# Weights loaded in double pieces, last stores moved behind a branch, and small start-up work moved between engines, in an RWKV-5 plus tanh-shrink kernel

## The chip, the cores and the metric

The program runs on one core of a Trainium2 chip. The core has five engines with queues of their own: TensorE (PE; its weight loads are shown as PEld), VectorE (DVE), ScalarE (ACT), GpSimd (POOL) and SyncE (SP). Loads and stores (DMAs) are issued from the queues of SP, ACT and POOL, and carried out by sixteen DMA engines that the queues share. The metric is the device time of one execution in microseconds (us), lower is better. A profile is of one execution, and its span is a little shorter than the execution's time.

## The reference

Two blocks follow each other. The first is a recurrence over 768 time steps for 4 batches and 8 heads of 48 columns; the second takes its output as 3072 tokens of 384 columns, multiplies by `w_in`, applies `h - tanh(h)`, and multiplies by `w_out`.

```python
state = np.zeros((B, H, D, D), dtype=np.float32)
for t in range(S):
    kt, vt, rt = (k[:, :, t], v[:, :, t], r[:, :, t])
    cur = np.einsum('bhd,bhe->bhde', u[None] * kt, vt)
    y[:, :, t] = np.einsum('bhd,bhde->bhe', rt, state + cur)
    state = w[None, :, :, None] * state + np.einsum('bhd,bhe->bhde', kt, vt)
x = np.ascontiguousarray(y.transpose(0, 2, 1, 3)).reshape(B * S, H * D)
h = x @ w_in                      # 3072x384 @ 384x2048
out = (h - np.tanh(h)) @ w_out    # 3072x2048 @ 2048x384
```

r, k, v, w and u arrive as 4-byte floats. The two weights arrive as 8-byte floats; the kernel receives them as 64-bit words and makes 4-byte floats of them itself.

## The kernel before

**The recurrence** is cut into 24 units: 12 chunks of 64 steps (`SHORT`), each for two pairs of batches. A unit (`unit(n)`) loads its r, k and v in two halves of 64 partitions each (L624), transposes r and k on PE into `x_ps` (L636), scales r by powers of the decay `w_up` (`scale_r`, L640), forms the products of r and k ("levels", L594), masks them into `at` (L771), and multiplies by v into `yk_ps` (L594). Between the chunks a state is carried: `keep` (L742, L744) puts in what the chunk adds, and a `decay` step (L780) multiplies it by the chunk's power of the decay. The first two units (`direct`) have their keys scaled by the inverse powers (`scale_k`, L644), read from `twice`, a copy of `inverse` with every power written out twice. The first unit takes its own term (the bonus u) from products with `kU` (L665); all later ones from the product of r and k and u, summed by DVE (L652, L765, L656).

**The start** loads w and u into `rows` (L536), transposes them (L538), and makes the tables `power`, `inverse`, `w_up`, `twice` and `w_down` (L541 to L550). `bounds` (L519) tests on DVE that every decay lies between 0.5 and 2.0; PE sums the test (L554), and the result is `flag`. If one does not, the whole output is computed again in another way by `anywhere`, which stands behind a branch at the program's end (L1124). With the data of the reference this branch is skipped, but every engine has to jump over the body.

**The dense block** is cut into 12 blocks of 256 tokens (`j`), each with 8 tiles of two columns of 128 (`hidden`). A tile is twelve matmuls for h (L165), five operations on ACT (L174 to L182), four on DVE (L189 to L195), and eight matmuls for the output sums o (L203). The first six blocks are gone through in four passes of four columns each, so that the first pass needs only a quarter of the weights; the partial sums are kept in `part` (L220, L211). The other six take all columns in one go.

**The weights** come in 32 pieces, by turns two of `w_in` (256 columns each) and two of `w_out` (two blocks of 128 rows each). `Weights.load` (L112) issues the loads of a piece: four for `w_in` (main rows for 48 partitions from SP, the rest for 16 partitions from POOL, each for two halves of the partitions) and one for `w_out`. A piece lands in a staging tile `st`, of which there are four, and `convert` (L122) makes 4-byte floats of it by seven steps, five on DVE (L134, L135, L138 to L140) and two on ACT (L136, L137).

**The order of the work** is not that of the code. Every step is added to a `Plan` with an engine, a cost that the author wrote down, and the steps it follows; loads also have a time for their data. `Plan.order` lays the steps out in time, walks back from the end for due times, and then tries 600 random shifts of the due times, keeping those that do not make the laid-out end later. Each engine then has its instructions in the fixed order that this gives. Where PE would stand idle early in that layout, `filled` puts in products that nobody reads (`fills`: L533 with 128 columns, L532 with 512). The layout also counts PE's instructions (`steps`, `CHUNK`, `CHUNK_0`): past certain counts it lets PE wait for more instructions.

**The end**: the last block's sums are copied by DVE into tiles `o` (L218), and each is stored in two halves, one issued from SP and one from ACT (L226); then comes the branch of L1124.

Of the kernel before, what the change touches and what calls it, by code (L numbers as in the profile page):

```python
# [30 lines left out]
SHORT = 64  # L31
# [3 lines left out]
L = 2  # L35
# [47 lines left out]
class Weights:  # L83

    COLS = 768

    def __init__(self, nc, stage, shared, moe_w_in, moe_w_out):
        self.nc, self.stage, self.d = nc, stage, shared["dims"]  # L90
        self.w_in_sb, self.w_out_sb = shared["w_in"], shared["w_out"]
        self.bias, self.sources = shared["p_bias"], (moe_w_in, moe_w_out)
        self.count = 2 * (self.d.NF // 2)
        self.staged = {}

    def piece(self, n):


        d, of = self.d, n // 4 * 2 + n % 2
        w_in, w_out = self.sources  # L100
        if n % 4 > 1:
            f = slice(2 * of, 2 * of + 2)
            return self.w_out_sb[:, f, :], [(slice(0, 128), w_out.rearrange("(ko ki) f -> ki ko f", ki=128)[:, f, :])]
        cols = w_in[:, of * 256 : (of + 1) * 256]
        parts = []
        for i in range(2):
            main = cols[: d.NK * 2 * d.D].rearrange("(k r) f -> r k f", k=d.NK)[i * d.D : (i + 1) * d.D]
            rest = cols[(2 * d.NK + i) * d.D :][: d.D].rearrange("(k x) f -> x k f", k=d.NK)
            parts += [(d.HEAD[i], main), (slice(i * PAD + d.D, (i + 1) * PAD), rest)]
        return self.w_in_sb[:, of], parts  # L110

    def load(self, n, i, queue):  # L112

        dst, parts = self.piece(n)
        if self.sources[n % 4 > 1].dtype == I64:
            if n not in self.staged:
                self.staged[n] = self.stage.tile([128, self.COLS], I64, name="st", tag="st", bufs=4)
            dst = self.staged[n].rearrange("p (k f) -> p k f", k=dst.shape[1])
        to, src = parts[i]
        queue.dma_start(out=dst[to], in_=src)  # L120

    def convert(self, n):  # L122

        V, A = self.nc.vector, self.nc.scalar
        dst = self.piece(n)[0].rearrange("p k f -> p (k f)")
        st = self.staged.pop(n)
        words = st.bitcast(U32).rearrange("p (n t) -> p n t", t=2)
        lo, hi = words[:, :, 0], words[:, :, 1]  # L130
        lo_f = st.bitcast(F32).rearrange("p (n t) -> p n t", t=2)[:, :, 0]
        power = self.stage.tile([128, self.COLS], U32, name="power", tag="power", bufs=2)
        bits = dst.bitcast(U32)
        yield V.tensor_scalar(power, hi, 0x7FF00000, None, ALU.bitwise_and)  # L134
        yield V.tensor_scalar(bits, hi, 0xFFFFF, 0x100000, ALU.bitwise_and, ALU.bitwise_or)  # L135
        yield A.activation(power, power, AF.Relu, scale=8.0, bias=self.bias)  # L136
        yield A.activation(lo_f, lo, AF.Copy, scale=2.0**-52)  # L137
        yield V.scalar_tensor_tensor(dst, bits, 2.0**-20, lo_f, ALU.mult, ALU.add)  # L138
        yield V.scalar_tensor_tensor(power, hi, 0x80000000, power, ALU.bitwise_and, ALU.bitwise_or)
        yield V.tensor_tensor(dst, dst, power.bitcast(F32), ALU.mult)  # L140


class Dense:


    def __init__(self, nc, work, gpool, ps_d, shared, out, rows, ps_o=None):
        self.nc, self.work, self.gpool, self.ps_d, self.ps_o = nc, work, gpool, ps_d, ps_o or (lambda: ps_d)
        self.out, self.rows, self.xts, self.sums = out, rows, {}, {}
        self.d, self.w_in_sb, self.w_out_sb, self.m1b, self.smallb = (
            shared[x] for x in ("dims", "w_in", "w_out", "m1b", "smallb"))  # L150
# [55 lines left out]
    def empty(self, t, i):  # L206
# [10 lines left out]
        if t.j == self.d.NB - 1:  # L217
            self.nc.vector.tensor_copy(t.o, self.outs[i])  # L218
        else:
            self.nc.scalar.copy(t.o, self.outs[i])  # L220
# [11 lines left out]
class Plan:  # L232
# [139 lines left out]
    def order(self, tries=600):  # L372
# [10 lines left out]
        chance = Random(3)  # L383
# [44 lines left out]
def near(ctx, tc, r, k, v, w, u, out, shared, weights):  # L428
# [15 lines left out]
    def fixed(name, shape, dt=F32):  # L444
# [6 lines left out]
                  lambda n: [(n % 2 * 2 + z) * d.S + n // 2 * SHORT for z in range(2)], lambda: later())  # L451
# [55 lines left out]
    power, inverse = (fixed(x, [128, NP, SHORT + 1]) for x in ("power", "inverse"))  # L507
    w_up, twice = (fixed(x, [128, NP, 2, SHORT]) for x in ("w_up", "twice"))
    w_down = fixed("w_down", [128, H, D])
    w_all = power[:, None, :, SHORT:].to_broadcast([128, 2, NP, D])  # L510
    ok, good = fixed("ok", [128, NP]), fixed("good", [128, 1])
# [7 lines left out]
    def bounds():  # L519

        V.tensor_scalar(ok, saved[:, :NP], W_LOW, None, ALU.is_ge)
        V.scalar_tensor_tensor(ok, saved[:, :NP], W_HIGH, ok, ALU.is_le, ALU.mult)
        V.tensor_reduce(good, ok, axis=mybir.AxisListType.X, op=ALU.add)
# [24 lines left out]
    doubled = add("DVE", .4, lambda: V.tensor_copy(twice, inverse[:, :, None, 1:].to_broadcast([128, NP, 2, SHORT])), [now])  # L548
# [3 lines left out]
    w_us = add("DVE", .1, lambda: V.tensor_tensor(w_u, saved[:, :NP], saved[:, NP:], ALU.mult), [keeps])  # L552
    now = add("DVE", .5, bounds, [keeps, doubled], 20)
    now = add("PE", .2, lambda: T.matmul(tab[0:1, 0:1], good, shared["one"], start=True, stop=True), [now, downs])  # L554
# [19 lines left out]
    loads, converted = [], []  # L574
    for n in range(weights.count):

        queues, data = (("SP",), (3.0,)) if n % 4 > 1 else (("SP", "POOL") * 2, (1.2, .8) * 2)
        of = [add(e, .55, lambda n=n, i=i, e=e: weights.load(n, i, e_of[e]), [converted[n - 4] if n >= 4 else None],
                  data=x, gated=True) for i, (e, x) in enumerate(zip(queues, data))]
        if weights.sources[n % 4 > 1].dtype != I64:  # L580
            converted.append(of[-1])
            continue
# [15 lines left out]
    def unit(n):  # L598
# [43 lines left out]
        def scale_k():  # L642
            t.kT = work.tile([128, NP, 2, SHORT], F32, name="kT", tag="kT")
            V.tensor_tensor(flat4(t.kT), k_ps, flat4(twice), ALU.mult)  # L644
# [94 lines left out]
        def keep():  # L739
# [3 lines left out]
            else:  # L743
                A.copy(now, kv_ps)  # L744
# [9 lines left out]
        if direct:  # L754
            x.kT = add("DVE", .62, scale_k, both + [doubled])
# [23 lines left out]
        x.add = add("DVE" if ch else "ACT", .47, keep, [x.out, x.rest, x.xt]) if more else None  # L779
        x.decay = add("DVE", .47, lambda: V.tensor_tensor(state[:, :, :, :D], state[:, :, :, :D], w_all, ALU.mult), [x.add]) if more else None  # L780
# [9 lines left out]
    def hidden(j, fs, f, due, pace):  # L790
# [28 lines left out]
        for i in range(L):  # L819
# [7 lines left out]
            if whole:  # L827

                by = ["SP", "ACT"] if j == d.NB - 1 else ["POOL"] * 2
                stored[j, i] = [add(by[z], .6, lambda z=z, i=i, ends=ends: dense.store(ends.o, L * j + i, z, e_of[by[z]]),  # L830
# [28 lines left out]
def anywhere(ctx, tc, r, k, v, w, u, out, shared):  # L859
# [199 lines left out]
    def last(t):  # L1059
        for z in range(2):  # L1060
            second.o(t, z)
        for i in range(L if t.last else 0):
            second.empty(t, i)
            second.store(t.o, L * t.j + i, 0, nc.sync)
# [25 lines left out]
def kernel(  # L1090
# [27 lines left out]
    shared = {"dims": d, "ident": ident, "w_in": w_in_sb, "w_out": w_out_sb, "flag": flag, **consts}  # L1118
# [5 lines left out]
    with tc.If(shared["far"] > 0):  # L1124
        anywhere(tc, r, k, v, w, u, out, shared)

# [30 lines left out]
```

## Time and profile before

| | before |
|---|---|
| time, median of 3 runs | 621.26 us (619.37 to 622.13) |
| profiled execution | 619.64 us, span 617.9 us |
| useful and other matmuls | 5211 PE rows, 601.9 us busy |
| DVE busy | 433.2 us (706 instructions) |
| ACT busy | 401.8 us (885) |
| POOL busy | 69.8 us (153) |
| weight loads from SP | 16 of `w_in` with 288 KB, 8 of `w_out` with 768 KB |
| weight loads from POOL | 16 of `w_in` with 96 KB |

Busy time is the time in which an engine carries out instructions; its share of the span does not say what a change in one stage is worth. For that one reads the stages: a table of windows gives busy time by engine for a stretch of the span, the timeline gives the instructions one by one with what they waited for, and the chain of waits is followed back from the last instruction, at each step to what released it. "issue" in the chain is time in which an engine waited for nothing that the profile shows.

### The profile page before, as it was taken

What the parts mean: (1) busy time and instruction counts of PE and PEld (TensorE: products, weight loads), DVE (VectorE), ACT (ScalarE), POOL (GpSimd) and SP (SyncE); (2) the same over time, 40 slices, a digit from 0 to 9 for tenths busy, and PEclk for the clock granted to TensorE, in tenths of its full rate; (3) what the DMA queues carried; (4) which work ended last, traced back from release to release, by engine and by line L of the source; (5) the groups of instructions that cost most, each with busy time, mean ns of one, the idle gap of its engine ahead of it and who ended that gap; (6) DMA issues with size and microseconds to landing.
All of it is one profiled execution on the core that took longest, in us unless ns stands there. A gap on an engine that the chain in (4) does not pass through costs nothing.

```text
span 617.9 us, 13049 instructions
## 1 busy us (share of the span) xinstructions
PE 601.9 (97%) x5211; PEld 444.5 (72%) x5211; DVE 433.2 (70%) x706; ACT 401.8 (65%) x885; POOL 69.8 (11%) x153
## 2 busy tenths in 40 slices
PE   8799999999999999999999999999999999999995
PEld 7476677777777777777677777777777777777772
DVE  6699977999689857996676665757556655555552
ACT  2497887887586657755665865756766576565551
POOL 4002113210001000002232011010010001110100
PEclk9899999999999999999999999999999999999999
DMA  6974446953006200001241221221101000100101
GB/s 130 185 163 90 83 88 115 221 110 103 2 19 107 79 0 2 0 12 40 62 90 38 40 46 27 40 47 27 39 20 25 16 14 9 26 7 2 27 1 31
DMA packets 86319, 33.69 MB, mean 55 GB/s; under 512 B 78536, under 2 KB 80680, under 8 KB 86248
## 3 DMA queue, kind: packets, MB, share of 16 engines
q1 hardware_dynamic: 81084, 25.57, 20.7%
q0 software_dynamic: 4992, 6.99, 5.1%
q8 instruction: 43, 0.70, 0.5%
q10 hardware_dynamic: 172, 0.20, 0.1%
q14 instruction: 28, 0.23, 0.1%
HBM read 26.94 MB, written 4.72 MB: 51 GB/s over the span
## 4 chain that ended last, share of the span: by engine, by line
PE 89%; DVE 5%; issue 2%; ACT 1%; DMA 1%; SPq 0%; POOL 0%; DVEq 0%; ACTq 0%; POOLq 0%
PE h L165 39%; PE o L203 38%; PE yk_ps L594 5%; PE x_ps L636 3%; PE x_ps L594 2%; PE h L533 1%; DMA rt<-in_r_dram 1%; PE h L532 1%; DVE rT L640 1%; DVE tg L193 1%; DVE rk L652 0%; DVE tg L191 0%; DMA vt<-in_v_dram 0%; DVE g L189 0%; DVE g L195 0%
## 5 line engine op out<-in xcount | busy, mean ns | idle before, releaser
L203 PE MATMUL o<-w_out_sb,g 128*128 128x384 f32 x768 | 280.4, 489 | 1.3 <-DVE g L195 1.3
L165 PE MATMUL h<-xt,w_in_sb 128*128 128x256 f32 x1152 | 280.1, 380 | 0.0
L165 PEld LDWEIGHTS h<-xt,w_in_sb 128*128 128x128 f32 x1152 | 216.4, 190 | 61.6
L203 PEld LDWEIGHTS o<-w_out_sb,g 128*128 128x128 f32 x768 | 142.8, 190 | 64.1 <-DVE g L195 2.6
L189 DVE TENSOR_TENSOR g<-h,th 128x512 f32<-128x512 f32 x96 | 66.1, 688 | 65.0 <-ACT s L174 41.6
L191 DVE SCALAR_TENSOR_TENSOR tg<-s,tg 128x512 f32<-128x512 f32 x96 | 66.0, 688 | 58.6 <-ACT tg L178 40.2
L178 ACT ACTIVATE tg<-h 128x512 f32<-128x512 f32 x96 | 57.1, 594 | 53.5 <-PE h L165 51.0
L174 ACT ACTIVATE s<-h 128x512 f32<-128x512 f32 x96 | 57.3, 597 | 48.3 <-PE h L165 48.3
L176 ACT ACTIVATE th<-h 128x512 f32<-128x512 f32 x96 | 57.2, 595 | 40.0 <-PE h L165 39.9
L195 DVE COPY_PREDICATED g<-small,tg 128x512 f32<-128x512 int32 x96 | 71.0, 741 | 5.0 <-ACT small L182 0.5
L193 DVE SCALAR_TENSOR_TENSOR tg<-q,tg 128x512 f32<-128x512 f32 x96 | 66.1, 689 | 9.3 <-ACT q L180 5.2
L182 ACT ACTIVATE small<-s,smallb 128x512 f32<-128x512 f32 x96 | 69.5, 724 | 0.5
L180 ACT ACTIVATE q<-s,m1b 128x512 f32<-128x512 f32 x96 | 69.5, 724 | 0.5
L736 POOL DMA_DIRECT2D xt<-rest x66 | 32.4, 498 | 206.3 <-ACT rest L722 206.0
L660 ACT ACTIVATE at<-same,du 128x64 f32<-128x64 f32 x184 | 47.8, 341 | 0.6 <-DVE du L656 0.3
L226 POOL DMA_DIRECT2D out_dram<-part x24 | 12.5, 526 | 125.3 <-DVE part L211 125.3
L720 ACT COPY xt<-yk_ps 128x192 f32<-128x192 f32 x22 | 7.1, 321 | 28.0 <-PE yk_ps L594 28.0
L211 DVE TENSOR_TENSOR part<-o,part 128x384 f32<-128x384 f32 x36 | 19.8, 551 | 4.2 <-PE o L203 4.2
L648 ACT COPY kT<-x_ps 128x512 f32<-128x512 f32 x22 | 12.9, 585 | 12.8 <-PE x_ps L636 9.4
L226 POOL DMA_DIRECT2D out_dram<-o x20 | 10.5, 531 | 91.1 <-ACT o L220 91.1
L771 DVE COPY_PREDICATED at<-before,x_ps 128x512 f32<-128x512 int32 x24 | 17.5, 728 | 4.5 <-PE x_ps L594 4.2
L594 PE MATMUL x_ps<-rT,kT 48*64 48x64 f32 x768 | 16.2, 221 | 4.6 <-issue 4.4
(101 smaller groups left out, 444.6 us busy)
## 6 DMA issues: line engine op xcount, KB each, us to landing
st<-in_moe_w_out_dram SPq DMA_DIRECT2D x8, 768.0 KB, 5.0
rt<-in_r_dram SPq DMA_DIRECT2D x48, 96.0 KB, 3.0
vt<-in_v_dram SPq DMA_DIRECT2D x48, 96.0 KB, 2.9
st<-in_moe_w_in_dram SPq DMA_DIRECT2D x16, 288.0 KB, 5.8
kt<-in_k_dram SPq DMA_DIRECT2D x44, 96.0 KB, 3.2
out_dram<-part POOLq DMA_DIRECT2D x24, 96.0 KB, 2.1
out_dram<-o POOLq DMA_DIRECT2D x20, 96.0 KB, 2.1
st<-in_moe_w_in_dram POOLq DMA_DIRECT2D x16, 96.0 KB, 5.9
```

Of the source, the lines that this page charges most:

```text
L165: self.nc.tensor.matmul(t.h2[:, z], self.w_in_sb[:, t.f // 2, kk, z * 128 : (z + 1) * 128], self.xts[t.j][:, kk].rearrange("p b t -> p (b ...
L174: A.activation(out, t.h, AF.Square)
L176: A.activation(out, t.h, AF.Tanh)
L178: A.activation(out, t.h, AF.Tanh, scale=G1)
L180: A.activation(out, t.s, AF.Square, bias=self.m1b)
L182: A.activation(out, t.s, AF.Relu, bias=self.smallb, scale=-1.0)
L189: V.tensor_tensor(t.g, t.h, t.th, ALU.subtract)
L191: V.scalar_tensor_tensor(t.tg, t.s, C4, t.tg, ALU.mult, ALU.mult)
L193: V.scalar_tensor_tensor(t.tg, t.q, K1, t.tg, ALU.add, ALU.mult)
L195: V.copy_predicated(t.g, t.small.bitcast(I32), t.tg)
L203: self.nc.tensor.matmul(self.outs[i], t.g2[:, z, i * C : (i + 1) * C], self.w_out_sb[:, t.f + z, :], start=t.first and z == 0, stop=t.last ...
L594: T.matmul(*args, skip_group_check=True, **how)
```

## The change

1. **Weights.** `load` now takes two pieces at once. A load of `w_in` covers 512 columns that lie in a row, and one of `w_out` four blocks of 128 rows. There are half as many loads, each twice as large, and two staging tiles of twice the size; a staging tile comes free when both its pieces are converted. Pieces are still converted one by one. The data times in the plan go from 1.2 to 2.0 (`w_in` main rows) and from 3.0 to 5.0 (`w_out`).
2. **Last stores.** The last block's sums go into a fixed tile `last` instead of `o`, and the four stores from it stand behind the branch, for both ways of computing. `anywhere` puts its own last rows into `last`.
3. **First states.** For the two first units of the recurrence, ACT's copy of the state and DVE's decay of it become four scaled copies on ACT.
4. **Tables.** `twice` is made by ACT instead of DVE, and `scale_k` reads `inverse` directly. `twice` and `inverse` take the buffers of other tiles.
5. **Bounds.** The test of the decays, and `w_u`, go from DVE to POOL, with two additions in place of a reduction.
6. **Order.** `Plan.order` makes 1000 tries instead of 600, from another seed. As the costs have changed too, the order on every engine differs.

```diff
     def load(self, m, i, queue):
-        dst, parts = self.piece(n)
-        if self.sources[n % 4 > 1].dtype == I64:
-            if n not in self.staged:
-                self.staged[n] = self.stage.tile([128, self.COLS], I64, name="st", tag="st", bufs=4)
-            dst = self.staged[n].rearrange("p (k f) -> p k f", k=dst.shape[1])
-        to, src = parts[i]
-        queue.dma_start(out=dst[to], in_=src)
+        to, src = self.parts(m)[i]
+        rows = src.shape[1]
+        if self.bits:
+            if m not in self.staged:
+                self.staged[m] = self.stage.tile([128, 2 * self.COLS], I64, name="st", tag="st", bufs=2)
+            queue.dma_start(out=self.staged[m].rearrange("p (k f) -> p k f", k=rows)[to], in_=src)
+            return
...
-        chance = Random(3)
+        chance = Random(5)
...
     def bounds():
-        V.tensor_scalar(ok, saved[:, :NP], W_LOW, None, ALU.is_ge)
-        V.scalar_tensor_tensor(ok, saved[:, :NP], W_HIGH, ok, ALU.is_le, ALU.mult)
-        V.tensor_reduce(good, ok, axis=mybir.AxisListType.X, op=ALU.add)
+        low, high = (ok[:, i] for i in range(2))
+        G.tensor_scalar(low, saved[:, :NP], W_LOW, None, ALU.is_ge)
+        G.tensor_scalar(high, saved[:, :NP], W_HIGH, None, ALU.is_le)
+        G.tensor_tensor(ok[:, 0], low, high, ALU.mult)
+        for n in (2, 1):
+            G.tensor_tensor(ok[:, 0, :n], ok[:, 0, :n], ok[:, 0, n : 2 * n], ALU.add)
...
-    doubled = add("DVE", .4, lambda: V.tensor_copy(twice, inverse[:, :, None, 1:].to_broadcast([128, NP, 2, SHORT])), [now])
+    doubled = add("ACT", .6, lambda: A.copy(twice, inverse[:, :, None, 1:].to_broadcast([128, NP, 2, SHORT])), [now])
...
             if ch:
                 V.tensor_tensor(now, kv_ps, now, ALU.add)
-            else:
-                A.copy(now, kv_ps)
+                return
+            for p in range(NP):
+                A.mul(state[:, :, p, :D], kv_ps[:, :, p], power[:, p, SHORT:])
...
-            if whole:
-                by = ["SP", "ACT"] if j == d.NB - 1 else ["POOL"] * 2
+            if whole and j < d.NB - 1:
...
     with tc.If(shared["far"] > 0):
         anywhere(tc, r, k, v, w, u, out, shared)
+
+    for b in range(d.B):
+        queue = (nc.sync, nc.scalar)[b % 2]
+        queue.dma_start(out=out[(b + 1) * d.S - SHORT : (b + 1) * d.S, :],
+                        in_=shared["last"][b % 2 * SHORT : (b % 2 + 1) * SHORT, b // 2, :])
```

## The prediction

> **What bounds the kernel now.** I read part 1 of the page first, then busy time by stage.
>
> ```profile
> PE 601.9 (97%) x5211; PEld 444.5 (72%) x5211; DVE 433.2 (70%) x706; ACT 401.8 (65%) x885; POOL 69.8 (11%) x153
> ```
>
> ```profile
> 0.00:15.00 15.00, 12.90 (x192) 11.73 (x195) 8.98 (x25) 3.92 (x9) 7.09 (x30) 1.00 0.65 128
> 15.00:30.00 15.00, 10.48 (x167) 6.66 (x158) 9.98 (x20) 6.54 (x18) 0.29 (x1) 0.89 1.07 188
> 30.00:45.00 15.00, 14.45 (x305) 11.48 (x304) 13.88 (x24) 14.21 (x35) 0.00 (x0) 1.00 0.81 171
> 45.00:60.00 15.00, 14.45 (x240) 10.17 (x239) 15.00 (x28) 11.08 (x36) 3.28 (x6) 1.00 0.43 82
> ...
> 600.00:618.00 18.00, 10.60 (x37) 6.41 (x35) 6.54 (x10) 4.45 (x8) 0.00 (x0) 0.92 0.10 27
> ```
>
> The columns are PE, PEld, DVE, ACT, POOL, granted clock, DMA share and GB/s. PE is the bound, but early on it is busy with filler products (L532, L533), so I counted useful work. The chain shows six h products in 1.29 us and four o products in 1.30: 1152 and 768 of them are 248 + 249 us; the small products and transposes add about 72. Of the 617.9 us span some 48 do no useful PE work: 32 by 60 us, 3 between 60 and 110, 5 to 6 up to 600, 1.6 at the last tile, 6.3 after the last product. In 30 to 60 us DVE works 28.9 of 30: there DVE sets the pace, later PE.
>
> The chain of waits shows the worst early loss:
>
> ```profile
> 16.13 0.38 PE x_ps L594 x9
> 16.51 4.44 issue
> 20.95 0.87 PE x_ps L594 x23
> 21.82 4.11 PE h L532 x6
> 25.93 0.45 PE h L533 x4
> ```
>
> PE stops inside one set of 32 products, waiting for no semaphore. The DMA records have one 16 KB packet of an instruction queue beginning at 18.04 (1.52 us): it is a wait for instructions. Then six fillers take 4.11 us, since the clock record is at half from 21.07 for 3.41 us.
>
> At the end, the timeline and the instructions of L1124 (the branch around `anywhere`):
>
> ```profile
> 610.46 0.56 DVE L218 COPY o<-o 128x384 f32<-128x384 f32 x1 [1.65 <-PE o L203]
> 611.05 1.79 SPq L226 DMA_DIRECT2D out_dram<-o  x2
> 611.05 1.78 ACTq L226 DMA_DIRECT2D out_dram<-o  x2
> 611.75 0.56 DVE L218 COPY o<-o 128x384 f32<-128x384 f32 x1 [0.73 <-PE o L203]
> ```
>
> ```profile
> L1124 SPq EVENT_SEMAPHORE  x8: 17/17/17, 613.4 to 616.2; - x8
> ...
> L1124 DVEq COMPARE_BRANCH  x1: 72/72/72, 611.8 to 611.8; - x1
> ...
> L1124 ACTq COMPARE_BRANCH  x1: 54/54/54, 612.9 to 612.9; - x1
> L1124 SPq COMPARE_BRANCH  x1: 50/50/50, 612.9 to 612.9; - x1
> L1124 DVEq EVENT_SEMAPHORE  x1: 21/21/21, 615.0 to 615.0; - x1
> L1124 ACTq EVENT_SEMAPHORE  x1: 17/17/17, 616.2 to 616.2; - x1
> ```
>
> SP and ACT branch only after their last store is issued. ACT is over the branch 3.3 us later, DVE 3.2. The last store landed at 615.32, but SP stood between its second and third semaphore from 613.48 to 615.85 and ACT arrived at 616.21; twelve waits and two barriers end the span at 617.93.
>
> [...] w_in, in groups of 48 partitions, moves at about 150 to 190 GB/s (its 2048 B packets take 176 ns each on 16 engines while queued), w_out over 128 partitions at 330 to 350. [...]
>
> **The change part by part.**
>
> *Stores behind the branch.* SP's queue is empty after its last load, so it branches some 60 us before the end; ACT branches after its last `small` (606.9) and is over it at 606.9 + 3.3 = 610.2, before the first copy ends at 611.0. The built program lets the four stores wait for the two copies alone. Issue and landing stay: 615.32. SP then has five waits left (0.06 each), a drain and the barriers (617.05 to 617.93): 615.32 + 0.3 + 0.13 + 0.88 = 616.6, against 617.93: **-1.3**. If the store lands sooner for want of fetches beside it, DVE's own branch (615.0) decides: -1.7. I take **-1.4**; nothing to -1.7 is the bound. Copying into `last` instead of `o` costs nothing: same size.
>
> *DVE's work before 35 us.* Away go `twice` (0.42), three bound operations (0.16 each), `w_u` (0.15) and two decays (0.56 each): 2.2 us. ACT gets `twice` (0.62, as L546, same shape) and, for two copies of 0.48, eight scaled copies; L660 (128x64) runs at 0.25 each, so 4 x 0.26 = 1.05 a state, 0.5 to 1.4 as bounds: +1.7 in all. In 15 to 30 us ACT is 6.5 of 15 busy and hides it; the second state falls where ACT is 14.2 of 15 busy, so 0.6 may show. POOL's six tiny operations, 0.1 (memset) to 0.3 (copy L692) each, end by 8.2; POOL waits until 8.83 for `vt` there, so its w_in loads, queued behind, are not held.
>
> *Before the stop.* `kT` no longer waits for `twice`: -0.45. But SP's order puts two loads of k (0.67 us each) ahead of `rows`, and PE transposes k first; that delays the decay chain by some 1.2, of which 0.68 is the wait for r that DVE had after the reciprocal. So kT begins at 10.02 + 1.2 - 0.68 - 0.45 = 10.1. DVE's next operation, the bonus product, now stands before both mask copies and waits for r of unit 1 (landed 12.15); unit 0's outputs stay near 14.0. **+0.1**, within 0.5.
>
> *The weights.* At the stop SP has issued 2 x 576 KB of w_in, not 2 x 288 KB; POOL's 384 KB are the same in two issues for four. PE's 220 rows before the stop are 220 in the new order too: it comes in the same set, after row 21 instead of 9. The fetch came behind the data queued before it was asked for, so it moves by the time of the extra 0.59 MB. At the rate then measured (173 GB/s over 12 to 18 us) that is +3.4; if 4096 B in a row go at w_out's 340 GB/s, twice the bytes take the old time: +0.1. [...] I take the middle, **+1.7**.
>
> *What follows it.* DVE's queue now has four conversion steps, `kw` and the bonus product, thus r of unit 2, before unit 1's mask copy; PE has four long fillers instead of three before the next transposes. From PE's restart F to the third `rT` on DVE: rest of the set 0.3, eight filler rows 5.1 (four at 0.86 while the clock is at half, four at 0.43), short fillers 0.4, transposes 0.9: F + 6.7, against 27.96 - 20.95 = 7.0 before. From there to the first g copy DVE has 22.3 us of spacing-priced work against 21.7 (0.47 for 384 columns, 0.61 to 0.65 for 512, 0.87 for conversions); before, 22.9 passed, 1.2 idle. With the same idle it ends at F + 30.2, where before had 50.86 - 20.95 = 29.9. So the 2.2 us saved are eaten by a longer DVE wait for the transposes: **+0.3**. PE's products up to the first o are the same in both orders (12 h, five level sets), fillers 11 long and 6 short against 11 and 9, so the delay stays.
>
> *w_out twice as big and later loads.* 1.5 MB in one go take 4.6 us instead of 2.3 in front of k and r of unit 3; these are wanted near 38 us and land near 33: hidden, 0 to 2.3 otherwise. Later weights load when PE has work from other blocks; 0.
>
> *Reordered middle.* PE loses 3 us from 60 to 110 while DVE is 82 to 90% busy; less DVE work earlier and another order can give some back. I take not quite half, -1.4; bounds -2.5 and +1.5.
>
> Sum: -1.4 + 0.1 + 1.7 + 0.3 - 1.4 = **-0.7** on the span of 617.9. That execution took 619.64 us; the three runs' median is 621.26, so the forecast is 621.26 - 0.7 = **620.6**.
>
> **Rivals.** *Faster:* DVE's savings reach PE. If the fetch moves by 0.1 alone and DVE's wait for the transposes is filled by conversions, 2.2 us come through, with 1.4 at the end and 0.9 in the middle: 0.1 - 2.2 - 1.4 - 0.9 = -4.4, 616.9. For it: DVE at 28.9 of 30; against it: filler products fixed in PE's queue. *Slower:* the doubled loads stand in front of everything asked for later, instructions above all. [...] if w_out's 2.3 us show too, with the end at -1.4 and nothing back in the middle: 3.4 + 0.1 + 0.3 + 2.3 - 1.4 = +4.7, 626.0. It decides once the fetch and w_out together cost over 4.1 us. *No effect of the stores:* [...] its 2.4 us stop stays and the end gains nothing: 620.6 + 1.4 = 622.0.
>
> **Numbers.** About 0.5% (3.1 us) is what a measurement of this kernel can tell from no change. No change 0.47 (0.07 of it with no gain at the end), faster 0.33, slower 0.20. The likeliest alone spans 618.2 to 624.3; four fifths of all, reaching into both other cases, 615.8 to 625.3.
>
> **What would show it.** In the new profile: PE's "issue" stop in the second level set, near 17 us and ending between 21 and 24.5 (right), or gone or before 20 (the fetch is not behind the data); [...] first o product near 53; ACT and SP branching before the copies, the span ending some 4.3 us after the last copy instead of 5.6. A first o product before 50 proves the DVE reckoning wrong; after 56, that of the loads.

## The result and the profile after

The changed kernel is slower. Its median was 624.80 us (624.24 to 625.33, 4 runs) where the kernel before had 620.35 on the same chip: ratio 1.0068, 95% interval 1.0039 to 1.0097, so +4.2 us (here and below, the times are medians; a ratio need not be that of the two medians, and the differences in us are taken from it). A second measurement (625.36 against 621.33) gave 1.0063, 1.0044 to 1.0081. The forecast was 620.6 with a range up to 625.3: the time lies in the range, but the kernel became slower where the forecast had it slightly faster.

Busy times, and three windows, from the start and the end (columns as before: PE, PEld, DVE, ACT, POOL, clock, DMA share, GB/s):

```profile
PE 604.6 (97%) x5209; PEld 444.8 (71%) x5209; DVE 434.9 (70%) x699; ACT 403.2 (65%) x892; POOL 66.6 (11%) x151
```

```profile
...
15.00:30.00 15.00, 11.64 (x137) 6.84 (x136) 8.34 (x15) 5.92 (x16) 0.27 (x1) 0.77 1.11 213
30.00:45.00 15.00, 13.37 (x259) 10.17 (x261) 14.45 (x25) 9.87 (x30) 0.00 (x0) 1.00 0.72 133
...
604.80:622.80 18.00, 12.29 (x42) 7.52 (x40) 7.38 (x12) 5.82 (x10) 0.00 (x0) 0.96 0.09 26
```

The sums hardly tell the two kernels apart. What does is the first row shown: from 15 to 30 us DVE is busy for 8.34 us where it was 9.98, at a granted clock of 0.77 where it was 0.89. The timeline of DVE in that stretch shows why; the figure in square brackets is the idle time before the instruction and what ended it:

```profile
13.61 0.56 DVE L675 TENSOR_TENSOR rk<-rt,first_k 128x384 f32<-128x384 f32 x1 [2.90 <-DMA rt<-in_r_dram]
...
18.52 0.14 DVE L576 TENSOR_SCALAR flag<-h 1x1 int32<-1x1 f32 x1
25.32 1.81 DVE L147 TENSOR_SCALAR power<-st 128x768 uint32<-128x768 uint32 x2 [6.66 <-DMA st<-in_moe_w_in_dram]
...
27.51 1.81 DVE L148 TENSOR_SCALAR w_in_sb<-st 128x768 uint32<-128x768 uint32 x2
...
29.70 0.72 DVE L795 COPY_PREDICATED at<-before,x_ps 128x512 f32<-128x512 int32 x1
...
30.77 0.68 DVE L662 TENSOR_TENSOR rT<-x_ps,w_up 128x512 f32<-128x512 f32 x1
```

The same instructions before:

```profile
18.59 0.56 DVE L134 TENSOR_SCALAR power<-st 128x768 uint32<-128x768 uint32 x1 [1.08 <-DMA st<-in_moe_w_in_dram]
19.07 0.55 DVE L135 TENSOR_SCALAR w_in_sb<-st 128x768 uint32<-128x768 uint32 x1
...
21.93 0.73 DVE L771 COPY_PREDICATED at<-before,x_ps 128x512 f32<-128x512 int32 x1
...
27.96 0.69 DVE L640 TENSOR_TENSOR rT<-x_ps,w_up 128x512 f32<-128x512 f32 x1 [2.19 <-ACT kT L648]
```

DVE stands for 6.66 us in front of the first conversion, which before found its data at 18.59. Behind it in DVE's queue come the second unit's mask copy (21.93 before, 29.70 now) and the third rT (the third unit's scaled r; 27.96 before, 30.77 now).

The conversion steps themselves have become slower too. The two that mask the words of a `w_in` piece took 0.56 and 0.55 us, and now take 0.95 each. In the doubled tile the 256 columns of one piece lie between those of the other, so that these two steps read in stretches; a piece of `w_out` still lies in one stretch, and its steps still take 0.56. Over the eight pieces of `w_in` (the weights come in 16 pieces in all, not 32) that is 5.9 us more work for DVE, more than the 2.2 us that the moved operations take away. The plan still counts 0.47 us for each of these steps. No run took this cost out alone.

The chain of waits for 9 to 38 us puts the whole stretch on one load:

```profile
11.17 13.96 DMA st<-in_moe_w_in_dram
...
25.22 0.05 DVEq L147
```

PE's stop for instructions, which the prediction moved to 21 to 24.5, is in the same set of products after 5 rows (9 before), and ends at 21.26 (20.95 before):

```profile
18.19 0.33 PE L616 MATMUL x_ps<-rT,kT 48*64 48x64 f32 x5
21.26 1.11 PE L616 MATMUL x_ps<-rT,kT 48*64 48x64 f32 x27 [2.75 <-issue]
22.31 6.29 PE L552 MATMUL h<-w_up,ident 128*128 128x512 f32 x8
```

Part 6 of both pages gives the loads from SP, with KB each and the median from issue to landing. Before:

```profile
st<-in_moe_w_out_dram SPq DMA_DIRECT2D x8, 768.0 KB, 5.0
...
st<-in_moe_w_in_dram SPq DMA_DIRECT2D x16, 288.0 KB, 5.8
```

and after:

```profile
st<-in_moe_w_out_dram SPq DMA_DIRECT2D x4, 1536.0 KB, 9.1
...
st<-in_moe_w_in_dram SPq DMA_DIRECT2D x8, 576.0 KB, 9.8
```

The end is as forecast. ACT and SP are past the branch before the copies, and the span ends 4.4 us after the last copy (618.4 to 622.8), where it was 5.6:

```profile
L1156 SPq COMPARE_BRANCH  x1: 45/45/45, 494.3 to 494.3; - x1
...
L1156 ACTq COMPARE_BRANCH  x1: 54/54/54, 612.0 to 612.0; - x1
L1156 ACTq EVENT_SEMAPHORE  x1: 17/17/17, 614.7 to 614.7; - x1
```

To compare stages I counted, as in the prediction, the time in which PE does no useful product: the length of a stretch less what its useful products need at the spacing in which they follow each other unhindered (0.215 us for h, 0.325 for o). By 60 us the changed kernel has lost 34.3 us where the kernel before had lost 32.0; from 60 to 130 it loses 7.0 for 3.1; from 130 to 600 nothing differs (5.7, 5.6); the end gives back 1.3. So +2.4 + 3.9 + 0.1 - 1.3 = +5.1, against 4.9 between the two profiled spans (the differences are of unrounded figures). A second profile of the changed kernel has 35.2 by 60 us, so a figure of one profile holds to about 1 us. The same count of every run below, in us:

```
                                       by 20  by 60  60-130  130-600
before                                  15.2   32.0     3.1     5.6
stores alone (old order)                15.2   32.4     3.2     5.4
moved operations alone (old order)      14.8   31.8     3.6     5.4
stores and moves (old order)            15.1   32.4     3.6     5.3
new seed alone                          15.3   34.1     6.4     5.9
doubled loads alone (old order)         15.2   37.5     7.6     7.2
doubled loads alone (searched)          15.2   36.6    10.6     8.0
whole change (old order)                15.2   35.0     6.6     6.1
whole change, single loads (searched)   15.2   36.1     3.9     5.9
changed kernel                          15.3   34.3     7.0     5.7
 its loads as two halves                15.3   33.1     7.0     6.0
 half of the first load                 14.8   28.1     6.8     5.8
 second-pass conversions held           15.3   34.8    12.0     5.8
 first conversions deferred             15.3   38.5     7.0     5.7
first load single (searched)            15.2   37.3     9.5     5.5
true data times (searched)              15.2   37.1    10.9     6.2
```

"Old order" and the indented rows keep every other instruction where the kernel before, or the changed kernel, has it; "searched" means that the plan was laid out anew.

### The profile page after: what moved, and what is told of

Its sections match the earlier page's. It is cut to its first block, busy times and chain, and to the rows that moved or that the text cites. A ratio compares the mean times of both kernels' runs of the same rounds, so it can differ in the third digit from the quotient of the medians.

```text
span 622.8 us, 12998 instructions
## 1 busy us (share of the span) xinstructions
PE 604.6 (97%) x5209; PEld 444.8 (71%) x5209; DVE 434.9 (70%) x699; ACT 403.2 (65%) x892; POOL 66.6 (11%) x151
## 4 chain that ended last, share of the span: by engine, by line
PE 80%; DVE 8%; DMA 3%; ACT 3%; issue 2%; SPq 2%; DVEq 0%; ACTq 0%
PE h L178 37%; PE o L216 36%; PE yk_ps L616 4%; DMA st<-in_moe_w_in_dram 2%; PE x_ps L658 2%; SPq L646 2%; PE x_ps L616 1%; DMA rt<-in_r_dram 1%; DVE g L202 1%; DVE rT L662 1%; DVE tg L204 1%; DVE power L152 1%; DVE g L208 1%; DVE power L147 1%; DVE w_in_sb L148 1%
## 5 line engine op out<-in xcount | busy, mean ns | idle before, releaser
L241 POOL DMA_DIRECT2D out_dram<-part x24 | 12.6, 528 | 149.2 <-DVE part L224 149.2
L616 PEld LDWEIGHTS yk_ps<-rT,state 48*64 48x64 f32 x704 | 12.3, 134 | 14.5 <-DVE state L765 7.4
L662 DVE TENSOR_TENSOR rT<-x_ps,w_up 128x512 f32<-128x512 f32 x24 | 16.4, 684 | 7.6 <-ACT kT L671 7.6
L616 PEld LDWEIGHTS yk_ps<-at,vt 64*64 64x64 f32 x752 | 13.2, 134 | 11.5 <-DVE at L795 5.7
```

The costliest lines, as they stand in the source:

```text
L616: T.matmul(*args, skip_group_check=True, **how)
```

## The experiments

My first theory was that the doubled loads cost the start and the newly found order the stretch from 60 to 130; the rival put all of it on the loads.

**The stores alone.** The four store tasks stay in the plan but issue nothing, so the order is kept; the copies go to `last`, and the stores stand behind the branch. To make room for `last`, `twice` takes another tile's buffer, as in the changed kernel. The main lines of the edit:

```diff
-                stored[j, i] = [add(by[z], .6, lambda z=z, i=i, ends=ends: dense.store(...
+                run = (lambda *x: None) if j == d.NB - 1 else dense.store
+                stored[j, i] = [add(by[z], .6, lambda z=z, i=i, ends=ends, run=run: run(...
```

> The kernel before with the last four stores alone moved behind the branch; the order of every other instruction is kept as it was. Branch theory: SP and ACT are over the branch before the copies, the span ends 4.4 us after the last copy instead of 5.6, so -1.2 to -1.4 us. Rival, that the stores land later or SP stops again behind them: 0, within 0.4.

Measured: 619.42 against 621.43, ratio 0.9967 (0.9955 to 0.9978): -2.0 us, a little more than expected. The mechanism is there, at the branch lines of this run:

```profile
L1137 ACTq COMPARE_BRANCH  x1: 54/54/54, 605.9 to 605.9; - x1
L1137 ACTq EVENT_SEMAPHORE  x1: 17/17/17, 608.5 to 608.5; - x1
```

In its one profile the span ends 5.1 us after the last copy, since that store landed 4.1 us after the copy, not 3.0. The other profiles with this edit show 4.2 to 5.5, those without it 5.6 to 6.1. The size rests on the timed runs.

**The whole change without the doubled loads**, order searched anew:

```diff
-            queues, data = (("SP",), (5.0,)) if m % 2 else (("SP", "POOL") * 2, (2.0, .8) * 2)
+        queues, data = (("SP",), (3.0,)) if n % 4 > 1 else (("SP", "POOL") * 2, (1.2, .8) * 2)
```

> The changed kernel with the loads of before (one piece each, four staging tiles, the old data times); everything else as changed, and the order is searched anew. Loads theory (the doubled loads cost both the 2.4 us lost by 60 us and the 3.9 lost from 60 to 130): what is left is the end, so 1.3 under the kernel before, about 619. Order theory (the loads cost only the 2.4; the rest is lost because conversions of the second pass now stand among the last steps of the recurrence, here after the ninth scale_r on DVE, where before they came after the twelfth): start as before, 60 to 130 still 2 to 4 worse, so 0.7 to 2.7 above the kernel before, about 622.

Measured: 620.96, ratio 0.9990 (0.9975 to 1.0004). Between both theories: 60 to 130 is nearly as before (3.9), but the start loses 36.1, more than the changed kernel. A new search moves the start by as much as the thing under test. The next two runs say the same more loudly.

**The doubled loads alone, searched anew:**

> The kernel before with the doubled loads alone. Loads theory: all of the loss without the gain at the end, +6, about 626. Order theory: in the order found here the second pass's conversions stand after the twelfth scale_r, as before, so only the start is lost: first w_in landing near 25 us, +2 to +3, about 623. Both expect the first w_in conversion near 25 us.

Measured: 633.60, ratio 1.0202 (1.0173 to 1.0231), +12.6 us: twice what the loads theory gave, and more than four times the other. **The seed alone:**

```diff
-    def order(self, tries=600):
+    def order(self, tries=1000):
-        chance = Random(3)
+        chance = Random(5)
```

> The kernel before with nothing changed but the search for the order: seed 5 and 1000 tries for seed 3 and 600. Loads theory: no change, within 0.6 of the kernel before. Order theory: the second pass's first conversion stands after the eleventh scale_r and not after the twelfth, so part of the loss from 60 to 130 appears without any change of the loads: +1 to +3.

Measured: 624.94, ratio 1.0057 (1.0040 to 1.0073), +3.5 us with no other change. So two runs of the same search, from another seed and with more tries, gave orders that differ by several us on the chip, and the one of the kernel before is the better. To price an edit, the order has to be held fixed. The next three runs do that.

**The doubled loads alone, old order.** A double load stands where the first of its two pieces was loaded, nothing where the second was.

```diff
-        of = [add(e, .55, lambda n=n, i=i, e=e: weights.load(n, i, e_of[e]), ...
+        of = [add(e, .55, lambda n=n, i=i, e=e: None if n % 2 else weights.load(n // 2, i, e_of[e]), ...
```

> The doubled loads alone, in the order of the kernel before: every other instruction stands in its old place, a double load stands where the first of its two pieces was loaded. Order theory (most of the slowing of the changed kernel comes from the order that the search finds, as the new seed alone cost 3.5): DVE meets the first conversion at 18.6 and waits for data until 22 to 25, which costs PE 1 to 3 us by 60 us and nothing later: +1 to +3. Loads theory (the loads cost what was lost, 6): +5 or more. Both ask whether 4096 B packets take 450 ns.

Measured: 630.99, ratio 1.0139 (1.0107 to 1.0170): +8.6 us. The order theory, that the loads cost 1 to 3, falls. Two places in this run's timeline hold the loss:

```profile
26.35 0.92 PE L607 MATMUL x_ps<-rT,kT 48*64 48x64 f32 x23 [8.49 <-issue]
...
124.57 0.95 DVE L147 TENSOR_SCALAR power<-st 128x768 uint32<-128x768 uint32 x1 [3.07 <-DMA st<-in_moe_w_in_dram]
...
128.49 1.92 PE L216 MATMUL o<-w_out_sb,g 128*128 128x384 f32 x4 [3.67 <-DVE g L208]
```

The stop for instructions has grown from 4.44 to 8.49 us and ends 5.4 later than before: the instruction packet begins at 23.47 instead of 18.04. And in the second pass DVE stands for a double load (10.65 us from issue to landing), with a tile's own `g` steps behind the conversion in its queue; PE waits 3.67 us for that `g`. By estimate 0.8 us of it is the slower conversion: two steps of 0.95 stand between the landing and that `g`. The two staging tiles are not what is late: this load was issued at 111.75, where before the first piece's was at 106.09, and the whole run is 5.4 us later by then.

**The moved operations alone, old order** (first states and `twice` on ACT, bounds and `w_u` on POOL):

> Parts 3, 4 and 5 alone (first states and twice on ScalarE, bounds and w_u on GpSimd), in the order of the kernel before, with single loads and the stores where they were. If DVE sets the pace early and 2.2 us of its work are gone: up to -1.5. If the fillers fixed on PE and the loads hide that: 0, within 0.7. Slower by over 0.7 only if the scaled copies on ScalarE (4 x 0.26 for 0.48) hold the second chunk.

Measured: 620.24, ratio 0.9989 (0.9977 to 1.0000): -0.7 us, at the edge of the noise. **The whole change, old order:**

> All of the change (doubled loads, stores behind the branch, moved operations), but in the order of the kernel before. Order theory: the sum of the parts at a fixed order, so -1.5 to +1.5 against the kernel before, and 3 to 5 under the changed kernel. Loads theory: as slow as the changed kernel, +4 or more.

Measured: 627.23, ratio 1.0098 (1.0074 to 1.0121): +6.1 us. The parts add: -2.0 - 0.7 + 8.6 = +5.9. So the change is slow in the old order too, and the new order is not what makes it slow. With the order of its own search the changed kernel stands some 2 us lower; the two intervals overlap, so that the new order wins something back is likely, not shown.

**Halves.** The changed kernel in its own order, each double load issued as two in a row:

```diff
-            queue.dma_start(out=self.staged[m].rearrange("p (k f) -> p k f", k=rows)[to], in_=src)
+            dst = self.staged[m].rearrange("p (k f) -> p k f", k=rows)[to]
+            for half in range(2):
+                at = ...
+                queue.dma_start(out=dst[at], in_=src[at])
```

> The changed kernel in its own order, but each double load issued as two loads one after the other at its place in the queue, of 256 columns (or two blocks of w_out) each, into the same staging tile; same bytes. If long rows help (4096 B in a row instead of 2048): slower by 1 to 3 than the changed kernel, for its first w_in would land later than 25.1. [...] packets of 2048 B take half of 450 ns, the landing stays within 1 us, and the time is that of the changed kernel within 0.8, +4.5 above the kernel before; more issues on SP (8 more in all at the start and middle) may cost a few tenths.

Measured: 623.23, ratio 1.0027 (1.0017 to 1.0036), so some 2 us faster than the changed kernel (1.0063 to 1.0068): neither theory had that, not the one that long rows help, nor the one that the landing and the time stay. The median packet of 2048 B took 209 ns, that of 4096 B 440 and 455 in the two profiles of the changed kernel, and from 13 to 22 us the traffic was 161 GB/s with halves and 160 and 156 without: here the longer rows moved no more bytes. The first conversion found its data earlier,

```profile
23.75 0.95 DVE L151 TENSOR_SCALAR power<-st 128x768 uint32<-128x768 uint32 x1 [5.41 <-DMA st<-in_moe_w_in_dram]
25.02 0.95 DVE L151 TENSOR_SCALAR power<-st 128x768 uint32<-128x768 uint32 x1 [0.32 <-DMA st<-in_moe_w_in_dram]
```

and later events came 1.2 to 1.6 us earlier, although PE's stop ended at 21.5, a little later than in the changed kernel. The second line shows why: the second piece's data were there only near 25.0, as late as the whole double load in the changed kernel (25.3). The bytes moved no faster; the first reader no longer waits for the half that it does not need. That pointed at the landing, not the end of PE's stop, as what binds in the changed kernel.

**The changed kernel again**, beside the next three:

> The changed kernel once more, beside the others of this call and as a second look at its place against the kernel before (+4.2 the first time) and against the version with halved loads (+1.7): +3.5 to +5. If it stands at +2 or below, the halves gained nothing.

Measured: 625.36, ratio 1.0063 (1.0044 to 1.0081), as expected.

**Half of the first load.** Its own order; the second 256 columns of `w_in` are left out (zeros, from one memset), which takes 768 KB of 1536 from the first load; the expectation misstates that amount.

```diff
+            some = slice(0, 256) if m == 0 else slice(None)
-            queue.dma_start(out=self.staged[m].rearrange("p (k f) -> p k f", k=rows)[to], in_=src)
+            queue.dma_start(out=self.staged[m].rearrange("p (k f) -> p k f", k=rows)[to][:, :, some], in_=src[:, :, some])
```

> The changed kernel in its own order, but the first w_in load brings only its first 256 columns (0.38 MB on SP and POOL together less than half of what it was); columns 256 to 511 of w_in are taken as zero, set by one early memset on DVE. This takes away the late landing and nothing else. Landing theory: the data are there near 18 to 20 instead of 25.1, DVE's wait of 6.7 us is gone for the most part, and PE loses 2 to 3 us less by 60 us: 2 to 3 under the changed kernel. Rival, that the fillers fixed on PE and DVE's pace hide the landing: within 0.7 of it.

Measured: 618.91, ratio 0.9964 (0.9952 to 0.9976): 6 us under the changed kernel, over twice what was expected. Its timeline:

```profile
17.80 0.68 PE L619 MATMUL x_ps<-rT,kT 48*64 48x64 f32 x27 [0.51 <-issue]
...
18.92 1.81 DVE L148 TENSOR_SCALAR power<-st 128x768 uint32<-128x768 uint32 x2 [1.48 <-DMA st<-in_moe_w_in_dram]
...
24.37 0.69 DVE L665 TENSOR_TENSOR rT<-x_ps,w_up 128x512 f32<-128x512 f32 x1
```

The conversion begins at 18.92 instead of 25.32, and the third rT at 24.37 instead of 30.77: the same 6.4 us, with the same 5.45 between them. The small PE stops of the changed kernel (86.5, 103.6, 112.2) are all there, 6.4 us earlier.

But the edit takes away more than the landing. PE's stop shrinks to 0.51 us, and the clock record has no half-speed stretch before the end, where the changed kernel has one of 6.83 us (20.74 to 27.56); the eight fillers behind the stop take 3.70 us instead of 6.29. So PE's own rows are 6.5 us earlier as well. Two chains meet at the third rT: DVE's, which hangs on the landing, and PE's, which ends with the transposes for it. In all profiles with this start:

```
                             conversion  transposes  third rT
                                 begins        done    begins
changed kernel                    25.32       29.92     30.77
 its second profile               26.19       29.96     31.64
 second-pass conversions held     25.88       29.31     31.34
 its loads as two halves          23.75       28.75     29.62
 half of the first load           18.92       23.43     24.37
 first conversions deferred       30.14       29.50     29.54
```

In the first three, which run the same instructions up to here, the third rT follows the conversion by 5.45 or 5.46 us, and the transposes by 0.85 to 2.0: the landing decides. But PE is close behind. An earlier landing alone could win 0.85 us in the first profile and 2.0 at most; the 6 us need both chains shorter, and the bytes of the double load stand behind both. Of the 5.45 us, 1.6 are the slower conversion steps (an estimate: four times 0.95 less 0.56); with the old duration PE's chain would be the later one in the first profile.

With half of the bytes gone, the order loses only 28.1 us by 60, which is 3.9 less than before. This is nearer to what the search laid out: it counted 2.0 us for the main rows of 576 KB, which at the measured 160 GB/s take 3.7.

**Second-pass conversions held back.** Its own order, the conversion steps of pieces 4 and 5 behind the twelfth unit's mask copy:

```diff
+        at = next(i for i, t in enumerate(order) if getattr(t, "unit", 0) == 11) + 1
+        held = [t for t in order[:at] if getattr(t, "piece", 0) > 3]
+        return [t for t in order[:at] if t not in held] + held + order[at:]
```

> The changed kernel in its own order, but the first steps of the second pass's conversions (pieces 4 and 5, four DVE steps of 0.87 in a row at 98.1 and the next two) are put behind the last mask copy of the twelfth unit. If they stand in the way of the recurrence: PE's stops at 103.6 and 112.2 go, 1 to 2 under the changed kernel. Rival, that the weights of the second pass are then late in their turn: within 0.7 of it, or up to 3 above, with a stop of PE before o near 125.

Measured: 630.12, ratio 1.0136 (1.0111 to 1.0160), worse than even the rival. PE's stop at 103.6 is gone, but

```profile
122.59 1.65 PE L216 MATMUL o<-w_out_sb,g 128*128 128x384 f32 x2 [3.96 <-DVE g L208]
```

stands where the old order had its stop. Here DVE waits for no load: the held conversion steps, from 113.97 on, stand in front of that `g`. The edit takes 0.9 us of loss from the stretch of 100 to 110 us and adds 5.8 from 110 to 130: the weights of the second pass are needed when the recurrence ends.

**A version that beats both**: old order, single loads, stores behind the branch, moved operations.

> The kernel before, in its own order and with single loads, with the stores behind the branch and the moved operations (parts 2 to 5 without the loads and the new search). The parts measured -2.0 and -0.7 alone. If they add: -2.7, about 618.6 where the kernel before stands at 621.3. If the moved operations were only noise: -2.0.

Measured: 618.95, ratio 0.9959 (0.9945 to 0.9973): -2.5 us.

Three more runs asked whether the late landing can be got round.

**First conversions deferred.** Its own order, the steps of pieces 0 and 1 behind the third scale_r and kT:

```diff
+        at = max(i for i, t in enumerate(order) if getattr(t, "unit", 0) == 2) + 1
+        held = [t for t in order[:at] if hasattr(t, "piece")]
+        return [t for t in order[:at] if t not in held] + held + order[at:]
```

> The changed kernel in its own order, all bytes loaded as there, but the first conversion steps of pieces 0 and 1 (four on DVE, three on ACT) stand behind the third scale_r and the third kT, so that the recurrence does not wait for the first double load; the instruction fetch and the landing stay as they were. If the place of the conversions in the in-order queues is what turns a late landing into lost time: third rT near 24 instead of 30.8, first h near 34.5 instead of 36.7, 1.5 to 3 under the changed kernel. If the fetch or the load's bytes set it: within 0.7 of it.

Measured: 627.96, ratio 1.0107 (1.0082 to 1.0133), slower by some 2 to 3 than the changed kernel. Neither theory holds, and the timeline tells why:

```profile
26.61 0.56 DVE L777 TENSOR_TENSOR kw<-kt,w_down 128x384 f32<-128x384 f32 x1 [9.21 <-DMA kt<-in_k_dram]
27.63 0.56 DVE L678 TENSOR_TENSOR rk<-rt,kt 128x384 f32<-128x384 f32 x1 [0.46 <-DMA rt<-in_r_dram]
...
29.54 0.69 DVE L665 TENSOR_TENSOR rT<-x_ps,w_up 128x512 f32<-128x512 f32 x1 [0.26 <-PE x_ps L661]
30.14 1.80 DVE L147 TENSOR_SCALAR power<-st 128x768 uint32<-128x768 uint32 x2
```

With the conversions out of the way DVE waits 9.21 us for k of the third unit, then for r. The recurrence's own inputs were issued behind the double load, and DVE has this k only at 26.61; the double load of the changed kernel had landed at 25.13 (11.17 + 13.96). So moving the conversions on DVE did not free it from that load. The third rT then waits for PE's transposes, and comes 1.2 us earlier than in the changed kernel, not 6; the conversions, from 30.14 on, are late for the first h product (38.72 for 36.71). Other profiles show the same: the changed kernel's v that was issued at 13.01 took 12.7 us to its landing, where the median of all v loads is 2.9 us, and the kernel with halves has in its chain a load of k that was issued at 12.80 and took

```profile
12.80 12.36 DMA kt<-in_k_dram
```

where the median of all k loads in the changed kernel is 3.1 us. What makes them so late was not shown. In the kernel before the second single piece is issued only behind this k and r (at 18.42; the two k issued from 12.08 on show 8.5 us to landing).

**The first load in single pieces, the rest doubled, searched anew:**

> The changed kernel with the very first w_in load in two single pieces (256 columns each, own tasks, old data times), every later load doubled; the order is searched anew. Landing theory: first conversion at 18.5 to 19.5, and the time is that of the changed kernel less about 5, so 1 to 3 under the kernel before. Rival, that doubled loads cost as much later on (two staging tiles, second pass): 2 or more above the kernel before.

Measured: 629.57, ratio 1.0140 (1.0113 to 1.0168). **True data times in the plan:**

```diff
-            queues, data = (("SP",), (5.0,)) if m % 2 else (("SP", "POOL") * 2, (2.0, .8) * 2)
+            queues, data = (("SP",), (5.0,)) if m % 2 else (("SP", "POOL") * 2, (3.6, 1.2) * 2)
```

> The changed kernel with the data times in the plan as the trace shows them (576 KB of w_in main rows 3.6 for 2.0, the rest from GpSimd 1.2 for 0.8) and nothing else; the order is searched anew, and still puts the four first conversion steps ahead of the second unit's mask copy. If a true price is all the search lacks: 2 to 4 under the changed kernel. If the search cannot use it: within 1.5 of the changed kernel.

Measured: 630.87, ratio 1.0150 (1.0112 to 1.0188). Neither helped. In the first, the data are there at 19.25, as expected, but PE's fixed fillers and its stop for instructions now bind:

```profile
21.93 0.92 PE L620 MATMUL x_ps<-rT,kT 48*64 48x64 f32 x24 [4.92 <-issue]
22.77 6.25 PE L553 MATMUL h<-w_up,ident 128*128 128x512 f32 x10
```

In the second it is a stop of 4.07 us and 18 fillers, 9.94 us in a row. Both lose 37 by 60 us and 9.5 and 10.9 from 60 to 130. These two say what the search makes of an edit, not what the edit costs.

## Why the prediction was wrong, step by step

By the count of PE's lost time the terms measured -1.3 for the end (forecast -1.4), +2.4 for the first 60 us (+2.1), +3.9 for the middle (-1.4) and +0.1 for the rest (0). So in numbers the miss is the middle, by 5.3 us; the first 60 us agree by chance, with wrong steps in them.

**The end, -1.4: right.** 4.4 us after the last copy as forecast, -1.3 in the profile of after, -2.0 (1.4 to 2.8) alone. SP branches 128 us before the end, not 60, which changes nothing.

**Before the stop, +0.1: the sum off by one landing.** kT began at 10.03 (forecast 10.1), and the bonus product stood before the mask copies as read from the order. But r of the second unit landed at 13.49, not at the 12.15 of before (12.2 to 13.2 in other runs of the same order). DVE waited 2.90 us, and unit 0's outputs came at 15.6 instead of 14.0. By 20 us a shorter stop had made up for it (15.3 lost, 15.2 before).

**The fetch, +1.7: mechanism right, size wrong here.** "It moves by the time of the extra 0.59 MB" fits where the order is kept: PE's restart comes 5.4 us later with the doubled loads in the old order, 3.3 later (22.79 for 19.52) when they are added to the moved operations there, and 3.5 earlier when 768 KB are taken from the changed kernel. At the changed order PE reached the stop 2 us later and the packet began at 18.30, so the restart moved by 0.3. Between the 173 GB/s measured from 12 to 18 us and the 340 of w_out the forecast took the middle; the lower rate was right (160 and 156 GB/s from 13 to 22 us).

**What follows it, +0.3: the step that failed first.** "From PE's restart F to the third rT on DVE ... F + 6.7" measured F + 9.5. Two things stand in its place. PE's own rows took 8.7: the clock was at half for 6.83 us, not for the 3.41 of the kernel before, so that the rest of the set and the eight fillers took 7.2 instead of 5.4. And when the transposes were done DVE was not: the last 0.85 us are its wait for the landing and the conversions behind it. The prediction names the four conversion steps ahead of the mask copy, but never asks when their data land, nor whether the doubled tile makes them slower. The doubled load was charged for what it delays in instructions, and not for itself, nor for the k and r queued behind it. An estimate was at hand: at the 173 GB/s that the prediction itself had measured, the 1.57 MB of that load take 9.1 us and the two loads of v and k that stand ahead of its last part (0.20 MB) 1.1. From the first issue at 9.1 that is 19.3 at the earliest, already past the 18.59 of before, with nothing counted that was queued ahead; it was 25.3. The run with half of the load puts 6 us on its bytes, through the landing and PE's stop together.

**"Later weights load when PE has work from other blocks; 0" and the reordered middle, -1.4: the term that was mis-sized.** It measured +3.9. In the old order the second pass's doubled loads cost PE a stop of 3.67 us and 4.5 in all. In the new one conversions stand among the recurrence's last steps, and holding them back brings a stop at the old place. They are in the chain of waits just ahead of PE's stop at 103.6:

```profile
98.14 1.80 DVE power L147 x2
99.94 1.72 DVE w_in_sb L148 x2
```

These four steps take 1.6 us more than at the old 0.56 each (an estimate), which is more than that stop of 0.94; no run tells how much of the 3.9 this is. That the doubled loads force this loss is not shown: the new seed alone, with single loads, loses 3.3 more there too, and the changed kernel without doubled loads only 0.8 more. That part stays open, as does whether some order exists in which doubled loads cost nothing.

The agreement by 60 us is chance (the second profile has +3.2 there): with half of the first load the new order is 3.9 better than the old one, and with all of it 6.3 worse than that.

**The rivals.** "The doubled loads stand in front of everything asked for later" (626.0) came closest, and its cause is the one shown; but what stood behind was the load itself, k and r as well as PE's instructions, and it has nothing of the middle. The faster rival's 2.2 us of DVE work did not come through: the moved operations gave 0.7, and the slower conversions put 5.9 back. "First o before 50 or after 56" was no test: it came at 53.99, as forecast, for another reason.

## What to carry to other kernels

The load that was made larger was itself later (9.8 us from issue to landing for 5.8, the medians of the `w_in` loads from SP), and so were loads behind it in the same queue (12.7 us for a v, where the median of the v loads is 2.9), and a reader of its first half waited for all of it (25.32, and 23.75 with halves). So before counting what a merged load saves in issues, write down its landing time at the rate that the profile shows for such loads (here 156 to 173 GB/s in the stretches between 12 and 22 us), and look for its first reader and the next loads in the queue. Ask also how the readers' steps change when the tile's layout does (0.56 to 0.95 us here). Where an order is searched, price each edit with the order held fixed; here a new seed and more tries alone moved the time by 3.5 us, nearly as much as the change. And a late landing was not cured by moving its reader back in its engine's order: the next reader's data came from the same queue (DVE stood 9.21 us for k), and another engine's chain ended almost as late (PE's transposes at 29.50).

## What the runs showed of the hardware

Rows of 4096 B in DRAM for 48 partitions moved no faster than rows of 2048 B: 440 to 455 ns a packet for 209, and 156 and 160 GB/s for 161. A DVE step over 768 words in each partition took 0.95 us where they lay in stretches of 256, with another piece's words between, and 0.56 where they lay in one stretch. The stop of PE for instructions in the same set of products took from 0.51 us (768 KB fewer in front) to 8.49 us (doubled loads, old order); after the first the clock record has no half-speed stretch there, after the second one of 10.24 us. PE went on 2.9 to 3.0 us after the beginning of the instruction packet (18.04 and 20.95 before, 18.30 and 21.26 in the changed kernel, 23.47 and 26.35 with doubled loads in the old order). SP's issue of a single load blocked for 5.03 us (the double w_out at 19.17 in the changed kernel) while the loads before it were still moving.
